# One more folded piece in the annex, eight more kept rows at the side, and a second pass in another order of groups and sizes (channel attention, 384x384x384)

## The chip, the cores and the metric

The kernel runs on one core of one Trainium2 chip. The metric is device time in microseconds (us) of one execution. Before the change: 716.69 us, the median of three runs (714.06, 716.69, 716.97).

## What is computed

The input `x` holds 384x384 positions of 384 channels in bf16 (113 MB). The reference takes the mean of each channel over all positions, multiplies it by the single weight `w1d[0]` (the 1D convolution has width k = 1), applies a sigmoid, and multiplies every position by the resulting 384 factors:

```python
g = jnp.einsum("bhwc->bc", x) / (H * W)
s = _sigmoid(g * w1d[0])          # k = 1: the loop over the window has one turn
return x * s[:, None, None, :]
```

The factors need all of `x`, so `x` must be read once in full before the first output can be written, and whatever cannot be held in on-chip memory must be read a second time.

## The kernel before

**Rows.** A "row" of the kernel is one position for each of the 128 partitions: 128 x 384 bf16, 98,304 bytes of HBM traffic when it is moved. `x` is 1152 rows. An instruction that the profile shows as 128x3072 works on 8 rows.

**Two passes.** Pass one loads all 1152 rows through the SP queue (`load`, L286) and lets TensorE add them into one PSUM bank (`sum_rows`, L292, a matmul with ones for each row). Of these, 392 rows stay on chip ("kept") and 760 are streamed: they pass through and are overwritten. ScalarE then makes the factors (`s_bf`, L516). Pass two scales the kept rows and stores them, loads the 760 streamed rows again, scales them (`scale`, L530, VectorE; three small pieces at the start on GpSimd) and stores them (`store`, L544). Loads and stores all go through the one SP queue, in program order.

**Memory.** The arena has 275 rows. A second area, the annex (20 rows, taken from the scratch of the descriptors), is numbered from X on. Before, the annex holds 20 raw kept rows, loaded at the start, and is only a buffer for streaming in pass two.

**Folding.** The exponent bits of the data have a small range, so the kernel packs 16 rows into the space of 12: `fold` (L343) takes pieces of 4 rows (three w and one u), moves the fields of u into unused bits of the three w, and frees the 4 rows of u. Each piece costs VectorE two tests (L359), four shifts and masks (`bits`, L327) and three joins (L333), and ScalarE two checks of 8 rows (L364). These share temporary rows (T and Y, 8 rows each), so one piece must finish before the next passes. The rows freed at the top of a group (U, V, W) and the temporary rows T and Y are loaded raw at the end of pass one. `unfold` (L548) takes a piece apart again in pass two: `fields` rebuilds u, `three` restores and scales the three w, `fourth` restores and scales u; both use T for halves. Pieces: FIRST (one), two columns of four groups of two pieces, BANKED (one piece of 6, whose words lie in PSUM banks during pass one) and EXTRA (one piece at A).

**Order.** In pass one, `BETWEEN` (L483) is written by hand: after which group which slots are streamed through; at L508 stands the order of the last raw loads. In pass two a planner runs while the program is built: it keeps a model clock and, by `RULES` (L650), `order` (L725) and the lists `landed` and `alongside`, decides at each moment whether VectorE unfolds a piece or scales landed rows, and when SP stores or loads, and how many rows at once. It writes a fixed sequence for each engine. On the chip a step waits only for what it needs: a load for the landing of the stores that free its rows, a store for its scaling, a scaling for the landing of its load. Since SP works in order, a waiting load also holds the stores behind it.

Of the kernel before, what the change touches and what calls it, by code (L numbers as in the profile page):

```python
# [145 lines left out]
def kernel(  # L146
# [13 lines left out]
    B, H, W, C = x.shape  # L160
# [5 lines left out]
    bf16, f32, u16, u32 = x.dtype, mybir.dt.float32, mybir.dt.uint16, mybir.dt.uint32  # L166
# [15 lines left out]
    ROWS = Y + 2 * PIECE  # L182


    FIRST = 0
    GROUPS = [(0, PIECE)]
    COLUMNS = ([FIRST], [])
# [11 lines left out]
    RING, SCRATCH = 1024, 16384  # L199
# [4 lines left out]
    X, N_X = ROWS + 1, (SCRATCH - RING) // (2 * C)  # L204
    END = X + N_X
    N_RAW = ROWS - W + 2 * PAIR + N_X
# [13 lines left out]
    arena = pool.tile([P, ROWS, C], bf16, name="arena")  # L220
# [22 lines left out]
    def mem(a, n):  # L243
        return arena[:, a : a + n, :] if a < X else annex[:, a - X : a - X + n, :]
# [8 lines left out]
    N_STREAM = RPP - N_RAW - 1 - sum(4 * q for _, q in GROUPS)  # L253
# [9 lines left out]
    r = N_STREAM + N_BANKED  # L263
# [7 lines left out]
    def raw(a):  # L271

        lo = a - U if a < G0 else PAIR + a - V if a < A else 2 * PAIR + a - W
        return c_raw + (lo if a < X else lo - (X - ROWS))
# [61 lines left out]
    def flat(a, p):  # L336
        return arena[:, a : a + p, :].bitcast(u16)
# [45 lines left out]
    N_DVE, N_SP = (62, 14), 27  # L383
# [45 lines left out]
    def take_raw(a, n):  # L429
        load(raw(a), a, n)  # L430
        return sum_rows(a, n)
# [7 lines left out]
    take_raw(X, N_X)  # L439
# [14 lines left out]
    SLOTS = [(A, 12), (A + 12, 12), (A + 24, 14)]  # L454
    S1, S2, S3 = ([slot] for slot in SLOTS)

# [8 lines left out]
    def group(g, where):  # L465
# [16 lines left out]
    LATE = [(W + 4, 8), (U, 8), (W + 12, 8), (W + 20, 7)]  # L482
    BETWEEN = [  # L483
        (2, LOW_COLUMN + HIGH), (4, [(A, 38)]),
        (5, [(G0 - 24, 24), (A - 24, 24), *S1]),
        (6, (S2, S3 + S1)), (7, ([(A - 24, 24)] + S2, S3 + S1)),
        (8, (S2 + S1, [(U, 8)] + S3)), (EXTRA, LATE),
    ]
# [59 lines left out]
    def unfold(g, lo, p, n, first, whole):  # L548

        a, at, m = first + 3 * lo, first + 3 * GROUPS[g][1] + lo, n * p  # L550
        folded = arena[:, a : a + 3 * m, :].rearrange("q (i j r) c -> q j i (r c)", i=n, j=3)
# [4 lines left out]
            arena[:, e : e + m, :].rearrange("q (i r) c -> q i (r c)", i=n).bitcast(u16)  # L556
# [64 lines left out]
    def again():  # L621
# [29 lines left out]
        (60, 190, 2.5, 14, 7.0, 5.0, 4.0),  # L651
        (150, 190, 2.5, 14, 5.0, 9.0, 3.0),
        (360, 72, 2.5, 33, 5.0, 7.0, 3.5),
        (N_STREAM, 220, 3.0, 14, 12.0, 7.0, 6.0),
# [43 lines left out]
    TOPS = {COLUMNS[0][-1]: U, COLUMNS[1][-1]: V, EXTRA: W}  # L698
# [11 lines left out]
    for a, n, end in ((Y, 2, True), (Y + 2, 2, True), (Y + 4, 4, True), (V, 4, True), (V + 4, 4, True), (T, 8, True), (X, 10, True), (X + 10, 10, True), (U, 8, True)):  # L710
        landed.append((a, raw(a), n, end))
    landed.append((W, raw(W), 8, True))
    landed.append((W + 8, raw(W + 8), 6, True))
# [14 lines left out]
    home[BANKED], home[EXTRA] = 2, 3  # L728
    free = [True] * 4
# [176 lines left out]
```

## Time and profile before

| | |
|---|---|
| profiled execution | 716.13 us |
| its span in the trace | 714.3 us |
| median of three runs | 716.69 us |
| moved by DMA | 301.34 MB, 422 GB/s over the span |
| HBM read / written | 187.96 / 113.25 MB |
| busy: PE / VectorE / ScalarE / GpSimd | 212.5 / 474.4 / 121.5 / 10.2 us |
| pass one ends (start of `s_bf`) | 268.65 us |
| first store of pass two issued | 269.85 us |

The 1.8 us between the profiled execution's time and its span lie outside what the trace shows. In the tables by windows each row gives, for 5 us, the busy time of each engine (with the number of instructions), then the granted clock of TensorE, the mean busy share of the 16 DMA engines and what they moved. The share can exceed 1.00 by a little, because packets are counted where they start.

### The profile page before, as it was taken

To read this page: it belongs to the slowest core of one execution; us is meant where nothing else is said; L and a number is where in the kernel's file an instruction comes from. 1 tells how busy PE (TensorE), PEld (TensorE's weight loads), DVE (VectorE), ACT (ScalarE), POOL (GpSimd) and SP (SyncE) were. 2 spreads that over 40 slices of the span, in tenths; PEclk is the share of its full clock that TensorE was granted. 3 is DMA by queue.
4 is the path that set the end of the run, shared out by engine and by line. 5 is a ranking of instruction groups with operands and counts; after the bars stand their busy time and mean duration, and the time that the engine had idled before them with its cause. 6 is when DMAs were issued, how large, how long until landed. Compare 5 with 4: busy or idle time off the path is not lost.

```text
span 714.3 us, 2033 instructions
## 1 busy us (share of the span) xinstructions
PE 212.5 (30%) x1186; PEld 0.3 (0%) x3; DVE 474.4 (66%) x350; ACT 121.5 (17%) x97; POOL 10.2 (1%) x7
## 2 busy tenths in 40 slices
PE   4768977997869780000000000000000000000000
PEld 0000000000000000000000000000000000000000
DVE  3605380639896827999989988999798388100960
ACT  3703260427675620000020000000000000000000
POOL 0000000000000005000000000000000000000000
PEclk9898989999999996555555555555555555555555
DMA  9999999999999998999999999999999999999997
GB/s 366 446 425 430 434 429 432 437 435 421 427 429 427 426 383 347 392 428 426 436 428 440 422 434 430 433 427 440 426 433 412 432 436 416 436 436 427 429 434 326
DMA packets 19454, 301.34 MB, mean 422 GB/s; under 512 B 2162, under 2 KB 2674, under 8 KB 7538
## 3 DMA queue, kind: packets, MB, share of 16 engines
q1 hardware_dynamic: 19440, 301.21, 99.0%
q8 instruction: 4, 0.07, 0.0%
q14 instruction: 8, 0.07, 0.0%
q10 hardware_dynamic: 2, 0.00, 0.0%
HBM read 187.96 MB, written 113.25 MB: 422 GB/s over the span
## 4 chain that ended last, share of the span: by engine, by line
DMA 69%; DVE 17%; PE 6%; ACT 2%; SPq 1%; issue 0%; DVEq 0%
DMA arena<-in_x_dram 47%; DMA out_dram<-arena 20%; DVE arena L530 11%; PE bank L292 6%; DVE arena L327 3%; ACT arena L364 2%; DVE annex L530 2%; DMA annex<-in_x_dram 2%; DMA out_dram<-annex 1%; DVE arena L333 1%; SPq L286 1%; ACT s_bf L516 0%; ACT bank L446 0%; DVEq L124 0%; SPq L901 0%
## 5 line engine op out<-in xcount | busy, mean ns | idle before, releaser
L530 DVE TENSOR_TENSOR arena<-arena,s_bf 128x4992 bf16<-128x4992 bf16 (+14 forms) x53 | 206.8, 3932 | 92.7 <-DMA arena<-in_x_dram 77.7
L292 PE MATMUL bank<-arena,ones 128*128 128x384 bf16 x1131 | 203.6, 341 | 46.3 <-DMA arena<-in_x_dram 45.6
L327 DVE TENSOR_SCALAR arena<-arena 128x1536 uint16<-128x1536 uint16 (+4 forms) x193 | 136.5, 761 | 109.0 <-DMA arena<-in_x_dram 93.9
L364 ACT ACTIVATE arena<-arena 128x3072 uint16<-128x3072 uint16 (+1 forms) x38 | 107.6, 2831 | 111.8 <-DVE arena L327 111.8
L333 DVE TENSOR_TENSOR arena<-arena 128x1536 uint16<-128x1536 uint16 (+3 forms) x81 | 106.3, 1312 | 9.9 <-PE bank L292 6.8
L610 PE MATMUL bank<-odd,ones 128*128 128x1 bf16 x1 | 0.2, 187 | 282.8 <-DVE odd L605 282.8
L446 ACT COPY arena<-bank 128x512 uint32<-128x512 uint32 (+3 forms) x9 | 4.5, 496 | 96.5 <-DMA out_dram<-arena 96.3
L530 DVE TENSOR_TENSOR annex<-annex,s_bf 128x3840 bf16<-128x3840 bf16 x8 | 16.9, 2152 | 1.9 <-DMA annex<-in_x_dram 1.9
L530 POOL TENSOR_TENSOR arena<-arena,s_bf 128x1536 bf16<-128x1536 bf16 (+1 forms) x3 | 10.0, 3352 | 269.2 <-ACT bank L520 269.2
L446 ACT COPY bank<-arena 128x512 uint32<-128x512 uint32 (+3 forms) x9 | 4.1, 490 | 26.4 <-PE bank L292 26.4
L530 DVE TENSOR_TENSOR arena<-arena,bank 128x1536 bf16<-128x1536 bf16 (+2 forms) x7 | 8.2, 1233 | 0.0
L364 ACT ACTIVATION_READ_ACCUMULATOR arena<-arena 128x1 f32 x38 | 7.1, 186 | 0.0
L292 PE MATMUL bank<-zeros,ones 128*128 128x384 bf16 x32 | 5.5, 326 | 0.0
L530 DVE TENSOR_TENSOR annex<-annex,bank 128x3840 bf16<-128x3840 bf16 x2 | 4.2, 2148 | 0.0
L292 PE MATMUL bank<-annex,ones 128*128 128x384 bf16 x20 | 3.4, 326 | 0.0
L516 ACT ACTIVATE s_bf<-bank,w_sc 128x384 bf16<-128x384 f32 x1 | 0.6, 581 | 13.6 <-PE bank L292 13.6
L306 PE MATMUL bank<-arena,ones 128*128 128x384 bf16 x1 | 0.5, 477 | 7.9 <-DMA arena<-in_x_dram 7.9
L874 ACT ACT_TABLE_LOAD x1 | 1.3, 1283 | 0.7 <-PEq L890 0.7
L396 DVE TENSOR_SCALAR w_sc<-bank 128x1 f32<-128x1 f32 x1 | 0.2, 159 | 1.1 <-PE bank L391 1.1
L386 DVE MEMSET ones<- 128x128 bf16 x1 | 0.2, 165 | 1.0 <-SPq L118 1.0
L391 PE MATMUL bank<-w_bf,ones 1*128 1x1 bf16 x1 | 0.2, 178 | 2.1 <-DMA w_bf<-in_w1d_dram 2.1
L614 DVE CAST odd_i<-bank 128x1 int32<-128x1 f32 x1 | 0.2, 158 | 0.3 <-PE bank L610 0.3
(11 smaller groups left out, 1.5 us busy)
## 6 DMA issues: line engine op xcount, KB each, us to landing
arena<-in_x_dram SPq DMA_DIRECT2D x16, 4608.0 KB, 30.6
out_dram<-arena SPq DMA_DIRECT2D x7, 4608.0 KB, 41.0
out_dram<-arena SPq DMA_DIRECT2D x7, 3072.0 KB, 25.1
arena<-in_x_dram SPq DMA_DIRECT2D x5, 3072.0 KB, 14.0
arena<-in_x_dram SPq DMA_DIRECT2D x13, 1152.0 KB, 18.6
arena<-in_x_dram SPq DMA_DIRECT2D x5, 2304.0 KB, 21.5
arena<-in_x_dram SPq DMA_DIRECT2D x3, 3744.0 KB, 18.9
out_dram<-arena SPq DMA_DIRECT2D x3, 3744.0 KB, 24.1
```

The lines of the kernel that those rows point to most:

```text
L286: lambda: nc.sync.dma_start(out=mem(a, hi - lo), in_=view(xf, *run)[:, lo:hi, :]),
L292: return pe.add_instruction(mybir.InstMatmult(name=nc.get_next_instruction_name(), ins=[pe.lower_ap(rhs), pe.lower_ap(ones[:])], outs=[pe. ...
L306: return nc.tensor.matmul(acc, lhsT=ones[:], rhs=mem(i, 1)[:, 0, :], start=first, stop=last)
L327: lambda: nc.vector.tensor_scalar(out=dst, in0=src, scalar1=s0, scalar2=s1, op0=op0, op1=op1),
L333: "DVE", lambda: nc.vector.tensor_tensor(out=dst, in0=a, in1=b, op=op), reads=reads, writes=writes
L364: lambda: nc.scalar.activation(out=y, in_=y, func=ACTF.Copy, accum_out=seen[:, 2 * k + i : 2 * k + i + 1]),
L386: fl.add("DVE", lambda: nc.vector.memset(ones[:], 1.0), writes=["ones"])
L391: lambda: nc.tensor.matmul(votes, lhsT=ones[0:1, :], rhs=w_bf[0:1, 0:1], start=True, stop=True),
L446: "ACT", lambda: nc.scalar.copy(dst.bitcast(u32), src.bitcast(u32)), reads=reads, writes=writes
L516: lambda: nc.scalar.activation(out=s_bf[:], in_=acc, func=ACTF.Sigmoid, scale=w_sc[:, 0:1]),
L530: lambda: vec.tensor_tensor(out=v, in0=v, in1=s[:, None, :].to_broadcast([P, n, C]), op=Op.mult),
L874: nc.scalar.preload_act_table(ACTF.Sigmoid)
```

## The change

It does three things.

1. A new folded group LATE: one piece (16 rows in 12) in the annex, at X, with its top at Z = X + 12; the last 8 rows of the annex are then raw kept rows. The annex is thereby no longer loaded at the start: in pass one it is a slot for streaming (three times all 20 rows), LATE's 16 rows come at the end, then the 8 raw ones.
2. EXTRA grows from one piece to two (32 rows in 24), so A to W holds 24 rows and its top at W has 8. Kept are 400 rows, streamed 752.
3. Pass two gets another order of groups, other first raw pieces (55 raw rows in place of 79), and other numbers in `RULES`. The streaming slots of pass one are cut anew, and SP's filler waits go from 27 to 26 pairs.

The core of the diff (three of the four rules are left out):

```diff
-    GROUPS.append((A, PIECE))
-    W = A + 3 * PIECE
+    GROUPS.append((A, PAIR))
+    W = A + 3 * PAIR
+    X, N_X = ROWS + 1, (SCRATCH - RING) // (2 * C)
+    LATE = len(GROUPS)
+    GROUPS.append((X, PIECE))
+    Z = X + 3 * PIECE
...
-    N_RAW = ROWS - W + 2 * PAIR + N_X
+    N_RAW = ROWS - W + 2 * PAIR + END - Z
...
-    take_raw(X, N_X)
...
-        (8, (S2 + S1, [(U, 8)] + S3)), (EXTRA, LATE),
+        (8, (S3, [(A + 12, 12), (W + 8, 7)])),
+        (EXTRA, (S3, [(U, 8), (V, 8), (W + 8, 7)])), (LATE, []),
...
-    for a, n in [(V, 8), *LATE, (W, 4), (T, 4), (T + 4, 4), (Y, 4), (Y + 4, 2), (Y + 6, 2)]:
+    for a, n in [(U, 8), (V, 8), (W + 8, 7), (W, 8), (Z + 4, 4), (Z, 4), (T, 4), (T + 4, 4), (Y, 4), (Y + 4, 2), (Y + 6, 2)]:
...
-        (60, 190, 2.5, 14, 7.0, 5.0, 4.0),
+        (45, 190, 1.5, 14, 12.0, 7.0, 5.0),
...
-    for a, n in ((A + 26, 4), (A + 30, 4), (A + 34, 5)):
+    for a, n in ((Z, 4), (Z + 4, 4), (W + 10, 5)):
...
-    order = [c0[-1], EXTRA, c0[-2], c0[-3], c1[-1], BANKED, c1[-2], c0[-4], c1[-3], FIRST, c1[-4]]
+    order = [c0[-1], c0[-2], c0[-3], c1[-1], c1[-2], EXTRA, c0[-4], FIRST, c1[-3], BANKED, LATE, c1[-4]]
```

The first place is SP's queue at the end of pass one, from the load of the last piece to be folded (128x6144, 16 rows) to the last load; f_PE, f_DVE and f_ACT name the engine that a load waits for. Before, that piece is EXTRA's; the first 128x1536 behind it is W (EXTRA's top), the next two are T, the last three Y:

```order
L286 DMA arena<-in_x_dram 128x6144 [waits f_PE]
L286 DMA arena<-in_x_dram 128x3072
L286 DMA arena<-in_x_dram 128x3072 [waits f_PE] x2
L286 DMA arena<-in_x_dram 128x2688 [waits f_PE]
L286 DMA arena<-in_x_dram 128x3072 [waits f_PE,f_DVE]
L286 DMA arena<-in_x_dram 128x3072 [waits f_PE] x3
L286 DMA arena<-in_x_dram 128x2688 [waits f_PE]
L286 DMA arena<-in_x_dram 128x1536 [waits f_DVE] x3
L286 DMA arena<-in_x_dram 128x1536 [waits f_ACT]
L286 DMA arena<-in_x_dram 128x768 x2
```

The same place after the change; the 16 rows are LATE's piece in the annex, the two annex loads of 128x1536 are the raw rows at Z + 4 and at Z (LATE's top), and the next two are T:

```order
L289 DMA annex<-in_x_dram 128x6144 [waits f_PE]
L289 DMA arena<-in_x_dram 128x3072 [waits f_PE] x2
L289 DMA arena<-in_x_dram 128x2688 [waits f_PE]
L289 DMA arena<-in_x_dram 128x3072 [waits f_DVE]
L289 DMA annex<-in_x_dram 128x1536
L289 DMA annex<-in_x_dram 128x1536 [waits f_PE,f_DVE]
L289 DMA arena<-in_x_dram 128x1536 [waits f_DVE] x2
L289 DMA arena<-in_x_dram 128x1536 [waits f_ACT]
L289 DMA arena<-in_x_dram 128x768 x2
```

Between the last piece to be folded and the first load that waits for its fold stood 70 rows (8, 8, 8, 7, 8, 8, 8, 8, 7, up to W); now 35 rows stand there (8, 8, 7, 8, 4, up to Z).

The second place is SP's queue early in pass two, from the last raw 128x3072 on; f_SP names the landing of an earlier transfer. Before:

```order
L544 DMA out_dram<-arena 128x3072 [waits f_DVE]
L544 DMA out_dram<-arena 128x2304 [waits f_DVE]
L286 DMA annex<-in_x_dram 128x7680 [waits f_SP18,f_SP20]
L286 DMA arena<-in_x_dram 128x4992 [waits f_SP16,f_SP19,f_SP22]
L544 DMA out_dram<-arena 128x4608 [waits f_DVE]
L286 DMA arena<-in_x_dram 128x3840 [waits f_SP23,f_SP0]
L286 DMA arena<-in_x_dram 128x3072 [waits f_SP14,f_SP15]
```

After:

```order
L545 DMA out_dram<-arena 128x3072 [waits f_DVE]
L545 DMA out_dram<-arena 128x768 [waits f_DVE]
L545 DMA out_dram<-arena 128x1920 [waits f_POOL]
L289 DMA annex<-in_x_dram 128x3072 [waits f_SP14,f_SP17]
L289 DMA arena<-in_x_dram 128x3072 [waits f_SP12,f_SP13]
L289 DMA arena<-in_x_dram 128x3072 [waits f_SP18]
L289 DMA arena<-in_x_dram 128x2688 [waits f_SP19,f_SP20]
L545 DMA out_dram<-arena 128x4608 [waits f_DVE]
```

The 128x4608 in both is the store of the first twelve unfolded rows. Ahead of it, 79 raw rows were stored and 33 loaded (20 and 13); now 55 are stored and 31 loaded (8, 8, 8 and 7).

The third place is VectorE at the start of pass two (L530 and L531 scale, L327 and L330 begin to unfold). Before:

```order
L530 TENSOR_TENSOR arena<-arena,s_bf 128x768 [waits f_PE,f_ACT]
L530 TENSOR_TENSOR arena<-arena,bank_72 128x768 [waits f_ACT]
L530 TENSOR_TENSOR arena<-arena,bank_72 128x1536 x3
L530 TENSOR_TENSOR arena<-arena,bank_72 128x3072
L530 TENSOR_TENSOR annex<-annex,bank_72 128x3840 x2
L530 TENSOR_TENSOR arena<-arena,bank_72 128x3072 x2
L530 TENSOR_TENSOR arena<-arena,s_bf 128x2304
L327 TENSOR_SCALAR arena<-arena 128x1536 [waits f_SP21]
```

After:

```order
L531 TENSOR_TENSOR arena<-arena,s_bf 128x768 [waits f_PE,f_ACT]
L531 TENSOR_TENSOR arena<-arena,bank_72 128x768 [waits f_ACT]
L531 TENSOR_TENSOR arena<-arena,bank_72 128x1536 x3
L531 TENSOR_TENSOR arena<-arena,bank_72 128x3072 x3
L531 TENSOR_TENSOR arena<-arena,bank_72 128x768
L330 TENSOR_SCALAR arena<-arena 128x1536 [waits f_SP16]
```

VectorE scales 42 raw rows in place of 66 before it unfolds the first piece. In the whole program the transfers through SP go from 135 to 144 (86 loads and 58 stores in place of 83 and 52), and the changes of direction between runs of loads and runs of stores from 21 to 33.

More of the change, by code (lines that the diff above doesn't have):

```diff
@@ L336, in flat @@
     def flat(a, p):
-        return arena[:, a : a + p, :].bitcast(u16)
+        return mem(a, p).bitcast(u16)
     SHL, SHR, AND, OR, XOR = (
@@ L453 @@
     PARTS = ((0, CUT, spare, "spare"), (CUT, C, tail, "bank0"))
-    SLOTS = [(A, 12), (A + 12, 12), (A + 24, 14)]
-    S1, S2, S3 = ([slot] for slot in SLOTS)
+    S1, S2, S3 = [(A, 19)], [(A + 19, 19)], [(X, N_X)]
     HIGH = [(A - 48, 48)]
@@ L550, in unfold @@
         a, at, m = first + 3 * lo, first + 3 * GROUPS[g][1] + lo, n * p
-        folded = arena[:, a : a + 3 * m, :].rearrange("q (i j r) c -> q j i (r c)", i=n, j=3)
+        folded = mem(a, 3 * m).rearrange("q (i j r) c -> q j i (r c)", i=n, j=3)
         w = [folded[:, j].bitcast(u16) for j in range(3)]
@@ L555, in unfold @@
         u, b, c = (
-            arena[:, e : e + m, :].rearrange("q (i r) c -> q i (r c)", i=n).bitcast(u16)
+            mem(e, m).rearrange("q (i r) c -> q i (r c)", i=n).bitcast(u16)
             for e in (at, HALVES, HALVES + m)
@@ L697 @@
     unused = set(range(HALVES, ROWS))
-    TOPS = {COLUMNS[0][-1]: U, COLUMNS[1][-1]: V, EXTRA: W}
+    TOPS = {COLUMNS[0][-1]: U, COLUMNS[1][-1]: V, EXTRA: W, LATE: Z}
     def stored(a, n):
@@ L707, in stored @@
         return f
[L710 to L713, printed above, removed]
+    for a, n in ((Y, 2), (Y + 2, 2), (Y + 4, 4), (V, 4), (V + 4, 4), (T, 8), (U, 8), (W, 8), (W + 8, 2)):
+        landed.append((a, raw(a), n, True))
     alongside = deque()
     t = 1.0
-    for a, n in ((A + 26, 4), (A + 30, 4), (A + 34, 5)):
+    for a, n in ((Z, 4), (Z + 4, 4), (W + 10, 5)):
         scale(a, n, "POOL", after=[copied])
@@ L724 @@
     (c0, c1), N_NEAR = COLUMNS, 2
-    order = [c0[-1], EXTRA, c0[-2], c0[-3], c1[-1], BANKED, c1[-2], c0[-4], c1[-3], FIRST, c1[-4]]
+    order = [c0[-1], c0[-2], c0[-3], c1[-1], c1[-2], EXTRA, c0[-4], FIRST, c1[-3], BANKED, LATE, c1[-4]]
     line = deque(order)
     home = {g: i for i, column in enumerate(COLUMNS) for g in column}
-    home[BANKED], home[EXTRA] = 2, 3
-    free = [True] * 4
+    home[BANKED], home[EXTRA], home[LATE] = 2, 3, 4
+    free = [True] * 5
     total = len(GROUPS)
```

18 lines of the change are left out of this document (8 added, 10 removed).

## The prediction

> **What bounds the kernel now.** I read the page's totals first, then the tables by windows, then the chain of waits and the timeline around the end of pass one. On the page:
>
> ```profile
> span 714.3 us, 2033 instructions
> PE 212.5 (30%) x1186; PEld 0.3 (0%) x3; DVE 474.4 (66%) x350; ACT 121.5 (17%) x97; POOL 10.2 (1%) x7
> DMA  9999999999999998999999999999999999999997
> q1 hardware_dynamic: 19440, 301.21, 99.0%
> DMA 69%; DVE 17%; PE 6%; ACT 2%; SPq 1%; issue 0%; DVEq 0%
> ```
>
> The 16 DMA engines carry packets for 99.0% of the span, 707 us of 714.3. No engine is above 66%. The 17% of VectorE in the chain is work beside a full queue: the DMA row shows a 9 almost everywhere. So what counts is the packets' time, plus the time in which the queue is empty. 301.21 MB in 707 us is 2.348 us per MB, or **0.231 us per row** of 98,304 bytes (3064 rows: 1152 read, 1152 written, 760 read again).
>
> Where is it empty? Stretches of the table by windows around the change of passes, then some of pass two:
>
> ```profile
> 255.00:260.00 5.00, 3.70 (x21) 0.00 (x0) 0.00 (x0) 0.03 (x1) 0.00 (x0) 1.00 1.02 424
> 265.00:270.00 5.00, 3.30 (x18) 0.00 (x0) 0.74 (x2) 0.90 (x2) 0.34 (x1) 1.00 0.30 115
> 270.00:275.00 5.00, 0.00 (x0) 0.00 (x0) 5.00 (x6) 0.00 (x0) 5.00 (x2) 0.70 0.83 328
> 275.00:280.00 5.00, 0.00 (x0) 0.00 (x0) 5.00 (x3) 0.00 (x0) 4.63 (x2) 0.50 1.02 424
> 280.00:285.00 5.00, 0.00 (x0) 0.00 (x0) 3.27 (x3) 0.00 (x0) 0.00 (x0) 0.50 1.03 428
> 285.00:290.00 5.00, 0.00 (x0) 0.00 (x0) 4.34 (x6) 0.00 (x0) 0.00 (x0) 0.50 1.03 382
> 295.00:300.00 5.00, 0.00 (x0) 0.00 (x0) 4.93 (x6) 0.00 (x0) 0.00 (x0) 0.50 0.99 345
> 320.00:325.00 5.00, 0.00 (x0) 0.00 (x0) 3.09 (x3) 0.00 (x0) 0.00 (x0) 0.50 1.00 423
> 440.00:445.00 5.00, 0.00 (x0) 0.00 (x0) 4.97 (x3) 0.00 (x0) 0.00 (x0) 0.50 1.01 435
> 445.00:450.00 5.00, 0.00 (x0) 0.00 (x0) 5.00 (x2) 0.00 (x0) 0.00 (x0) 0.50 1.01 435
> 550.00:555.00 5.00, 0.19 (x1) 0.10 (x1) 1.50 (x4) 0.00 (x0) 0.00 (x0) 0.50 1.00 374
> 595.00:600.00 5.00, 0.00 (x0) 0.00 (x0) 2.19 (x2) 0.00 (x0) 0.00 (x0) 0.50 0.81 317
> ```
>
> Between the passes the shares of 0.30 and 0.83 leave 3.50 + 0.85 = **4.35 us** empty. Beside that, four windows carry less than the 430 GB/s or so of the rest: 382, 345, 374 and 317, which is 0.6 + 1.0 + 0.7 + 1.3 = **3.5 us** lost. In three of them the share is about 1, so there the packets themselves take longer; nothing on an engine explains it.
>
> **The change part by part.**
>
> *Fewer rows.* 752 instead of 760 rows are read twice: 8 x 0.231 = **-1.85 us**. The page would show 300.42 MB instead of 301.21 on the main queue.
>
> *Nine more transfers* (144 instead of 135). Each has 128 packets, 8 per DMA engine. The window from 275 to 285, with transfers of 4 to 10 rows, moved 424 GB/s at a share of 1.02 and 428 at 1.03, so 2.41 us of packets per MB; 440 to 450, with long ones, 435 at 1.01: 2.32. The 0.09 us per MB go with about 200 packets per MB (some 5 KB each) instead of about 33 (30 KB), a difference of 10 per engine, so about 8 ns per packet. 9 x 8 x 8 ns = **+0.6 us**.
>
> *Two more folds in pass one*, with their 13-odd VectorE instructions and two ScalarE tests each. The last fold of before from the timeline, the end of pass one from the chain, and SP's first stores from the timeline (first column start, second duration):
>
> ```profile
> 247.22 1.90 DVE L327 TENSOR_SCALAR arena<-arena 128x3072 uint16<-128x3072 uint16 x3 [1.01 <-DMA arena<-in_x_dram]
> 252.17 2.76 ACT L364 ACTIVATE arena<-arena 128x3072 uint16<-128x3072 uint16 x1 [1.10 <-DVE arena L327]
> 252.99 1.94 DVE L333 TENSOR_TENSOR arena<-arena 128x1536 uint16<-128x1536 uint16 x2
> ```
>
> ```profile
> 267.15 1.47 PE bank L292 x8
> 268.63 0.02 issue
> 268.65 0.59 ACT s_bf L516
> 269.24 0.02 issue
> 269.26 5.28 DVE arena L530 x6
> ```
>
> ```profile
> 269.85 5.05 SPq L544 DMA_DIRECT2D out_dram<-arena  x7
> ```
>
> A fold lasts 247.22 to 254.93, **7.7 us**; its last look at the u rows ends where the two joins begin, after 5.8 us. That was hidden: 70 rows, 16.2 us of packets, lay between EXTRA's piece and the load at W, and VectorE was idle from 255 to 260. Now 35 rows, 35 x 0.231 = 8.1 us, lie between LATE's piece and the load at Z that waits for 5.8 us of its fold. To that comes the delay from last packet to seen landing and from issue to first packet. The change of passes gives the two together: 4.35 us empty, of which 267.15 to 269.85 (PE, ScalarE, first scaling), 2.7 us, is work; **1.65 us** is left. 5.8 + 1.65 = 7.45 < 8.1: Z comes in time by 0.65 us. The end of the fold releases the second half of T: 7.7 + 1.65 = 9.35 against 8.1 plus the 8 rows of Z and T (1.85) = 9.95. So no hole, if the fold starts when its piece lands. If VectorE is still at EXTRA's second piece, the hole grows one for one; that piece lands 39 rows (9.0 us) earlier and takes 7.7, so 1.3 us are in hand. I take **+0.1**, with 0 and +1.3 (a backlog of twice that slack) as ends. For the fold before, in the middle of the pass, other queued streams are the cover.
>
> *The first stores of pass two.* The order is now: 55 raw rows, loads of 31, then the first twelve unfolded rows. The last raw scaling and the first piece taken apart, from the timeline:
>
> ```profile
> 281.92 1.35 DVE L530 TENSOR_TENSOR arena<-arena,s_bf 128x2304 bf16<-128x2304 bf16 x1
> 285.59 1.50 DVE L327 TENSOR_SCALAR arena<-arena 128x1536 uint16<-128x1536 uint16 x3 [2.31 <-DMA out_dram<-arena]
> 287.12 1.95 DVE L333 TENSOR_TENSOR arena<-arena 128x1536 uint16<-128x1536 uint16 x2
> 288.99 1.35 DVE L327 TENSOR_SCALAR arena<-arena 128x4608 uint16<-128x4608 uint16 x1
> 290.38 2.56 DVE L530 TENSOR_TENSOR arena<-arena,s_bf 128x4608 bf16<-128x4608 bf16 x1
> ...
> 292.96 0.34 SPq L544 DMA_DIRECT2D out_dram<-arena  x1
> 293.40 0.86 SPq L286 DMA_DIRECT2D arena<-in_x_dram  x2
> 293.44 0.96 DVE L530 TENSOR_TENSOR arena<-arena,s_bf 128x1536 bf16<-128x1536 bf16 x1
> ```
>
> The piece takes 7.4 us from its start to its first store, 8.8 us (285.59 to 294.40) for its 16 rows. It started 2.31 us after VectorE was free, when the store of U's 8 rows had landed. Walk through the new order: packets resume near 271; 86 rows (55 stored, 31 loaded) keep the queue busy for 19.9 us, to 291. VectorE scaled 66 raw rows from 269.26 to 283.3, 0.21 us per row; 24 fewer take 5 us less, so it is free near 278.3. U's rows are then stored 36 rows into the queue and no longer 60 (24 x 0.231 = 5.5 us earlier, 280 at best); I take 282 for the start, since they are also scaled in between. Its twelve rows are issued near 289.5 and have packets about 1 us later, 290.5. That is 0.5 us in hand. From there a single piece costs VectorE 8.8, and the scaling of 16 rows loaded in its place 16 x 0.21 = 3.4, together 12.2 us; DMA needs 48 rows x 0.231 = 11.1. Each such piece drains the queue by 1.1 us; the first two groups, now four pieces (before: three), are taken so, later ones as pairs, which cost less. The loads that SP issues ahead refill it. I take **+0.2 us** of holes; the ends are 0 and the missing reserve, 24 rows x 0.231 = +5.5.
>
> *More changes of direction*, 33 instead of 21. Four slow windows (3.5 us) stand against 17 changes that cost nothing visible (320 to 325, with loads of 20 and 13 rows turning to stores: 423). In proportion it would be 12 x 3.5/21 = +2.0. But 595 to 600 lies within a run of long loads, so the link is weak; by the nearest rows, most are free. I take **+0.6**; the ends are -2.5 (the slow places not met) and +2.0.
>
> *Nothing:* the later BANKED group (its copies are on ScalarE, which is 17% busy); two filler waits less on SP (behind them lie some 6 us of queued loads); the first load, now without the annex (140 rows, 32 us, are queued before a load waits for TensorE); the final three loads and stores (43 rows at the end in both).
>
> Sum, against the profiled execution's 716.13: -1.85 + 0.6 + 0.1 + 0.2 + 0.6 = -0.35, so **715.8 us**. The median of the runs shown is 716.69, 0.56 above that execution, and one run is 2.6 below it; what a measurement of this kernel can tell from no change is about 0.5%, or 3.6 us. The term that the change is sure of is half of that.
>
> **The rivals.**
>
> *Early drought.* VectorE is the bound of the first 60 us of pass two. For it: 0.5 us in hand at 291 and 12.2 against 11.1 us; SP is in order, so a store that waits for a scaling holds the loads behind it, and VectorE waits for those. Against it: before, the same piece had 2.3 us to spare. It decides from the point where a piece with its reload takes over 11.1 us for more than two pieces in a row without a reserve. Price up to 5.5 us less what I took: 721.1. Slower.
>
> *Every change of direction costs*, in proportion: +1.4 on my sum, 717.2. Within 0.5%.
>
> *Every transfer pays its delay.* If the 1.65 us between packets and their neighbours were not covered for the nine added transfers, they would cost 9 x 1.65 = 14.9 instead of 0.6 us: 730.1. Slower. The window 275 to 285, with transfers of 0.4 to 1 MB at 424 to 428 GB/s, speaks against it: behind a full queue the delay does not show. The Trainium skill (DMA: Bandwidth & Descriptors, section Bandwidth) has this rule, to batch transfers to 1 MiB or more for 75% of peak; its section on the anatomy of a DMA puts the fixed part at about 2 us, by which the nine would be an estimated 18 us. By that rule the smaller transfers of pass two are a mistake; the trace disagrees as long as others are queued.
>
> *The slow places vanish.* They may be accidents of where reads and writes meet, and the new order meets elsewhere: -2.5 instead of +0.6, so 712.7. Faster. Against it: more places to meet.
>
> *The change does not do what it says:* if the bytes did not fall by 0.79 MB, the sum would be 717.6.
>
> **How the numbers follow.** My forecast with its near neighbours 0.77 (of these 0.15 for direction in proportion and 0.01 for the bytes); drought 0.14; a delay per transfer 0.01; vanishing slow places 0.08. So faster by over 0.5% 0.08, within 0.77, slower 0.15. The range reaches most of the vanishing below, 713.2, and the larger part of the drought above, 719.5; about 0.12 is left out.
>
> **What would show it.** The main queue carries 300.4 MB. The window with the end of LATE's fold shows a DMA share of 1; a share under 0.8 there means that Z waited. The change of passes stays near 4.35 us. Between 285 and 345 the shares stay near 1: if they fall to 0.9 or lower in several windows and SP's waits for VectorE's scaling grow, it is drought. If shares stay at 1 and GB/s falls below 400 in more than four windows, it is direction. Wrong would be the whole argument if the span moved by more than 3 us with the sum of packets and holes unchanged.

## The result and the profile after

The change makes the kernel slower: 718.75 us, the median of 20 runs (715.95 to 723.41), against 716.59 (714.06 to 717.89, 20 runs) before; the ratio is 1.0042 with the 95% interval 1.0028 to 1.0055, so +2.2 us; 715.8 us was forecast. The profiled execution of after took 722.76 us, 4 us over its median; where a number needs it, two more profiles of after (717.42 and 717.46 us) and a second of before (717.80) stand beside it.

The page of after, the same rows that the prediction shows of before:

```profile
span 721.0 us, 2103 instructions
PE 217.6 (30%) x1186; PEld 0.3 (0%) x3; DVE 500.4 (69%) x394; ACT 132.8 (18%) x105; POOL 10.2 (1%) x7
DMA  9999999999999997999999999999999999999997
q1 hardware_dynamic: 20736, 300.43, 98.7%
DMA 61%; DVE 24%; PE 10%; ACT 1%; SPq 0%; issue 0%; DVEq 0%
```

The bytes are those of the forecast (300.4 MB). The row of tenths looks almost as it did, and the busy share of the queue is a little lower (98.7% after 99.0%). In the chain the DMA's part fell by 8 points while VectorE's and TensorE's grew; that alone says little, since the fastest kernel of this record (deeper_full, below) has 55% for the DMA and 30% for VectorE. The windows of after, around the end of pass one and the start of pass two (the last three numbers are TensorE's clock, DMA share and GB/s):

```profile
245.00:250.00 5.00, 3.78 (x15) 0.00 (x0) 4.71 (x8) 3.69 (x4) 0.00 (x0) 0.73 1.01 425
250.00:255.00 5.00, 5.00 (x30) 0.00 (x0) 4.06 (x6) 2.86 (x2) 0.00 (x0) 0.93 1.03 415
255.00:260.00 5.00, 4.06 (x26) 0.00 (x0) 4.92 (x8) 3.59 (x3) 0.00 (x0) 1.00 0.85 263
260.00:265.00 5.00, 3.84 (x23) 0.00 (x0) 4.76 (x7) 3.90 (x3) 0.00 (x0) 1.00 1.01 414
265.00:270.00 5.00, 4.37 (x27) 0.00 (x0) 0.96 (x1) 1.07 (x2) 0.00 (x0) 1.00 1.01 367
270.00:275.00 5.00, 2.57 (x14) 0.00 (x0) 0.00 (x0) 0.35 (x1) 0.00 (x0) 1.00 0.37 139
290.00:295.00 5.00, 0.00 (x0) 0.00 (x0) 3.46 (x3) 0.00 (x0) 0.00 (x0) 0.50 0.88 327
295.00:300.00 5.00, 0.00 (x0) 0.00 (x0) 4.87 (x5) 0.00 (x0) 0.00 (x0) 0.50 1.02 338
```

In before, 255 to 260 moved 424 GB/s; here it moves 263. The chain of after in order of time (start, duration, what) says what the last loads of pass one waited for:

```profile
265.02 0.97 DVE annex L336
265.99 0.02 issue
266.01 0.33 SPq L289
266.34 0.04 issue
266.38 6.71 DMA arena<-in_x_dram
273.08 0.04 issue
273.13 1.50 PE bank L295 x8
274.63 0.02 issue
274.65 0.59 ACT s_bf L517
```

The last join of LATE's fold ends at 265.99, and 20 ns later SP issues a load that waited for it. From there a straight line leads to the factors at 274.65, 6.0 us later than in before (268.65). The chain names only the last link; the window that lost most, 255 to 260, lies ahead of it. In the two further profiles of after the factors start at 271.09 and 272.37, in that of before at 269.01.

What stands behind the factors: 721.0 - 274.65 = 446.35 us, and 444.5 and 443.3 in the other two; in before 445.65 and 447.0. By the means of these five profiles **pass one loses 3.9 us and pass two gains 1.6**. The sum, +2.3, is near the measured loss, but the parts are rough: the three profiles of after lie up to 3.6 us apart in pass one and 3.0 in pass two.

### The profile page after: what moved, and what is told of

Read it like the earlier page. It is cut to its first block, busy times and chain, and to the rows that moved or that the text cites. A ratio compares the mean times of both kernels' runs of the same rounds, so it can differ in the third digit from the quotient of the medians.

```text
span 721.0 us, 2103 instructions
## 1 busy us (share of the span) xinstructions
PE 217.6 (30%) x1186; PEld 0.3 (0%) x3; DVE 500.4 (69%) x394; ACT 132.8 (18%) x105; POOL 10.2 (1%) x7
## 3 DMA queue, kind: packets, MB, share of 16 engines
q1 hardware_dynamic: 20736, 300.43, 98.7%
## 4 chain that ended last, share of the span: by engine, by line
DMA 61%; DVE 24%; PE 10%; ACT 1%; SPq 0%; issue 0%; DVEq 0%
DMA arena<-in_x_dram 45%; DVE arena L531 17%; DMA out_dram<-arena 13%; PE bank L295 10%; DVE arena L330 4%; DMA annex<-in_x_dram 3%; DVE arena L336 2%; ACT arena L367 1%; DMA out_dram<-annex 1%; DVE annex L531 0%; DVE annex L336 0%; SPq L289 0%; DVE annex L330 0%; SPq L545 0%; ACT s_bf L517 0%
## 5 line engine op out<-in xcount | busy, mean ns | idle before, releaser
L531 DVE TENSOR_TENSOR arena<-arena,s_bf 128x6144 bf16<-128x6144 bf16 (+10 forms) x68 | 220.1, 3269 | 83.0 <-DMA arena<-in_x_dram 72.6
L330 DVE TENSOR_SCALAR arena<-arena 128x1536 uint16<-128x1536 uint16 (+4 forms) x205 | 143.5, 754 | 94.9 <-DMA arena<-in_x_dram 85.5
L295 PE MATMUL bank<-arena,ones 128*128 128x384 bf16 x1067 | 194.6, 345 | 39.8 <-DMA arena<-in_x_dram 39.2
L367 ACT ACTIVATE arena<-arena 128x3072 uint16<-128x3072 uint16 (+1 forms) x42 | 118.6, 2824 | 111.6 <-DVE arena L330 111.6
L336 DVE TENSOR_TENSOR arena<-arena 128x1536 uint16<-128x1536 uint16 (+3 forms) x87 | 112.8, 1296 | 14.3 <-PE bank L295 11.3
L295 PE MATMUL bank<-annex,ones 128*128 128x384 bf16 x84 | 17.8, 377 | 7.5 <-DMA annex<-in_x_dram 7.5
L531 DVE TENSOR_TENSOR annex<-annex,s_bf 128x3072 bf16<-128x3072 bf16 (+1 forms) x4 | 8.6, 2156 | 2.9 <-DMA annex<-in_x_dram 2.8
L531 POOL TENSOR_TENSOR annex<-annex,s_bf 128x1536 bf16<-128x1536 bf16 x2 | 6.2, 3108 | 275.2 <-ACT bank L521 275.2
L531 DVE TENSOR_TENSOR arena<-arena,bank 128x1536 bf16<-128x1536 bf16 (+2 forms) x8 | 8.6, 1144 | 0.0
L330 DVE TENSOR_SCALAR arena<-annex 128x1536 uint16<-128x1536 uint16 (+1 forms) x9 | 4.9, 599 | 0.2
L336 DVE TENSOR_TENSOR annex<-annex,arena 128x1536 uint16<-128x1536 uint16 (+1 forms) x4 | 4.6, 1156 | 0.2
L531 POOL TENSOR_TENSOR arena<-arena,s_bf 128x1920 bf16<-128x1920 bf16 x1 | 3.8, 3827 | 0.0
L309 PE MATMUL bank<-arena,ones 128*128 128x384 bf16 x1 | 0.5, 477 | 7.7 <-DMA arena<-in_x_dram 7.7
L330 DVE TENSOR_SCALAR annex<-annex 128x1536 uint16<-128x1536 uint16 (+1 forms) x3 | 2.5, 820 | 0.0
```

Of the source, the lines that this page charges most:

```text
L295: return pe.add_instruction(mybir.InstMatmult(name=nc.get_next_instruction_name(), ins=[pe.lower_ap(rhs), pe.lower_ap(ones[:])], outs=[pe. ...
L309: return nc.tensor.matmul(acc, lhsT=ones[:], rhs=mem(i, 1)[:, 0, :], start=first, stop=last)
L330: lambda: nc.vector.tensor_scalar(out=dst, in0=src, scalar1=s0, scalar2=s1, op0=op0, op1=op1),
L336: "DVE", lambda: nc.vector.tensor_tensor(out=dst, in0=a, in1=b, op=op), reads=reads, writes=writes
L367: lambda: nc.scalar.activation(out=y, in_=y, func=ACTF.Copy, accum_out=seen[:, 2 * k + i : 2 * k + i + 1]),
L531: lambda: vec.tensor_tensor(out=v, in0=v, in1=s[:, None, :].to_broadcast([P, n, C]), op=Op.mult),
```

## Experiments

Six questions, seventeen runs. A name that begins with p1 is a kernel without pass two: after the factors it scales and stores two rows and ends. "Rows on their way" at the issue of a load are the rows of all loads issued before it that have not landed. They are worked out from the start of each issue and from the completions in the trace, 16 to a load (one from each DMA engine), counted in order of time, whichever load they belong to. One row is 0.231 us of packets.

### Which pass loses?

`p1_before` and `p1_after` are the two kernels without pass two.

> The kernel before with pass two left out: after the factors, two rows are scaled and stored, and nothing else. It gives pass one's length alone. In the profile before, the factors begin at 268.65 us; the first scaling, one store and the end add some 6 us, so about 276 us. All theories expect the same here; the run is the base for the next two.

> The changed kernel with pass two left out in the same way. Theory A (the loss is made in pass one, where the changed streaming slots and the late fold leave SP's queue so shallow that DMA engines which are out of step run dry): longer than the kernel before without pass two by 2 to 6 us. Theory B (the loss is made in pass two, by more changes of direction and smaller transfers): within 0.7 us of it.

Measured: 275.30 us (274.70 to 275.68) and 277.56 us (276.70 to 278.84). The isolated pass one loses 2.3 us, less than the mean of the three profiles of whole kernels (3.9). That the loss lies ahead of the factors, both say; how much pass two gives back, they do not agree on: by these medians 0.1 us (718.75 - 277.56 against 716.59 - 275.30), by the profiles 1.6.

### Is it the size of the streaming slots?

`p1_fine` and, whole, `fine_full` cut the three slots of the change in two:

```diff
-    S1, S2, S3 = [(A, 19)], [(A + 19, 19)], [(X, N_X)]
+    S1, S2, S3 = [(A, 10), (A + 10, 9)], [(A + 19, 10), (A + 29, 9)], [(X, 10), (X + 10, 10)]
```

SP's filler waits go from 26 to 22 pairs with it.

> The changed kernel without pass two, and with the streaming slots of pass one cut in two (10 and 9 rows instead of 19, 10 and 10 instead of 20; six more loads, SP's filler waits down by four pairs to keep the same place). Theory A1 (the size of the slots is what makes TensorE and SP wait): at least 1 us shorter than the changed kernel without pass two. Theory A2 (LATE's fold, which now ends the pass, is what counts): no shorter than that, within 0.7 us. Theory B: all three within 0.7 us.

> The changed kernel with the streaming slots of pass one cut in two, and pass two unchanged. Theory A1: at least 1 us faster than the changed kernel, 716.5 to 717.5. A2 and B: as the changed kernel, 718 to 719.5.

Measured: 277.78 us (276.51 to 279.53), no better than the change; whole, 717.40 us, ratio to before 1.0018 (1.0005 to 1.0031). The whole kernel lies in theory A1's range, but its interval overlaps that of the change (1.0028 to 1.0055), and its pass one alone is not shorter, so the sizes are not shown to be a cause. (Nor did six more transfers cost anything like a delay of 1.65 us each.)

### Is it one place?

Four kernels. `p1_cover` streams 19 rows once more ahead of a load that waits at 213 to 219 us; `p1_nolate` leaves out LATE's fold; `p1_bless` was to take the rows at that first place out of before; `p1_early` loads and folds LATE at the start and has the slots of before.

```diff
-        (2, LOW_COLUMN + HIGH), (4, [(A, 38)]),
+        (2, LOW_COLUMN + HIGH), (4, [(A, 19)]),
...
-        (6, (S1, S2)), (7, ([(A - 24, 24)], S1)),
+        (6, (S1, S2)), (7, ([(A - 24, 24)] + S2, S1)),
```

That is p1_cover, against the change; p1_nolate, against the change:

```diff
-                fold(k)
+                if g != LATE:
+                    fold(k)
```

p1_bless, against before:

```diff
-        (2, LOW_COLUMN + HIGH), (4, [(A, 38)]),
+        (2, LOW_COLUMN + HIGH), (4, [(A, 38), (A, 19)]),
...
-        (6, (S2, S3 + S1)), (7, ([(A - 24, 24)] + S2, S3 + S1)),
+        (6, (S2, S3 + S1)), (7, ([(A - 24, 24)], S3 + [(A, 5)])),
```

And p1_early, against the change:

```diff
     take(BANKED)
+    take(LATE)
+    take_raw(Z + 4, 4)
...
+    for k in of_group(LATE):
+        fold(k, TEMPS, TEMPS + 2 * GROUPS[BANKED][1])
...
-    S1, S2, S3 = [(A, 19)], [(A + 19, 19)], [(X, N_X)]
+    S1, S2, S3 = [(A, 12)], [(A + 12, 12)], [(A + 24, 14)]
...
-        (6, (S1, S2)), (7, ([(A - 24, 24)], S1)),
-        (8, (S3, [(A + 12, 12), (W + 8, 7)])),
-        (EXTRA, (S3, [(U, 8), (V, 8), (W + 8, 7)])), (LATE, []),
+        (6, (S2, S3 + S1)), (7, ([(A - 24, 24)] + S2, S3 + S1)),
+        (8, (S3 + S1, [(U, 8)] + S2)),
+        (EXTRA, ([(U, 8), (W + 8, 7)], [(U, 8), (V, 8), (W + 8, 7)])),
```

Its last raw loads begin with four rows at Z, since Z + 4 is loaded at the start.

> The change's pass one alone (pass two left out: two rows scaled and stored), with the slot S2 (19 rows) streamed once more in group 7, ahead of the load that waits for the sums of a 24-row stretch, and 19 rows less after group 4; the same 1152 rows in all. The change without this edit took 277.56 us, the kernel before 275.30. Theory C (queue too short at 215 to 230 us, between the 24-row load and the 8-row load that waits for its sums: 43 rows in the change, 62 here as before): 276.2 to 276.8. Theory F (the wait for LATE's fold at the end costs it all): 277.3 to 277.8. If each has its part: 276.5 to 277.2, with a share near 1 from 215 to 230 us.

> The change's pass one alone (pass two left out), and LATE's sixteen rows are loaded and summed but not folded (that work is left out), so that the last loads wait for EXTRA's fold, 8 us earlier. Theory F (the wait for LATE's fold at the end costs it all): 275.3 to 275.8. Theory C (the short queue at 215 to 230 us): 277.2 to 277.8. If each has its part: 276.2 to 277.0, with 255 to 265 us at a share near 1 and 215 to 230 us as low as it was.

> The pass one of before alone (pass two left out), with S2 (19 rows... 12 in this kernel's slot plus 7) taken out ahead of the waiting load in group 7, so that 43 rows stand there as in the change, and 19 rows more after group 4. Without the edit 275.30 us. Theory C: 276.0 to 276.8, with a share under 1 near 215 to 230 us. Theory F: 275.1 to 275.6, since the end of pass one is untouched.

> The change's pass one alone (pass two left out), with 400 kept rows as in the change, but LATE's sixteen rows loaded and folded at the start of the program and the annex not used for streaming; the slots and their order as before (12, 12 and 14 rows). Theories C and F both: 275.2 to 275.8, as before, since neither the short queue nor the late fold is left. A third (the extra fold itself, 8 us more of VectorE in pass one, or the 24 more rows in folds, costs the time wherever it stands): 277.0 to 277.8.

Measured: 278.22 (277.42 to 278.69), 277.73 (276.82 to 279.20), 283.6 (282.65 to 285.02) and 278.01 us (277.19 to 278.64). Neither single place brought anything back: p1_nolate came out in theory C's range, but p1_cover, which was to settle C, is slower than any theory gave it. p1_early, where both theories forecast the time of before, was as slow as the change. So for a while the third theory (the extra fold costs the time wherever it stands) was ahead. The windows of p1_early pointed elsewhere:

```profile
245.00:250.00 5.00, 3.98 (x23) 0.00 (x0) 4.89 (x8) 3.69 (x3) 0.00 (x0) 1.00 0.98 372
250.00:255.00 5.00, 3.35 (x20) 0.00 (x0) 4.81 (x6) 3.97 (x3) 0.00 (x0) 1.00 0.97 385
255.00:260.00 5.00, 3.63 (x21) 0.00 (x0) 3.90 (x7) 3.05 (x4) 0.00 (x0) 1.00 0.93 318
260.00:265.00 5.00, 2.31 (x14) 0.00 (x0) 0.00 (x0) 0.00 (x0) 0.00 (x0) 1.00 0.92 333
```

The time is lost at the end of pass one, as in the change, though LATE's fold is at the start. What is left there is EXTRA's second piece and its slots U, V and W + 8, each used again soon after its last use. So it is not one place: every kernel of this group has some load that waited and was issued with few rows on their way.

p1_bless was badly made, since its second use of A stands directly behind the first, but its windows show the pure case:

```profile
160.00:165.00 5.00, 4.22 (x26) 0.00 (x0) 4.61 (x7) 3.79 (x3) 0.00 (x0) 1.00 0.95 402
165.00:170.00 5.00, 3.30 (x21) 0.00 (x0) 4.64 (x6) 3.80 (x4) 0.00 (x0) 1.00 0.03 12
170.00:175.00 5.00, 3.04 (x19) 0.00 (x0) 3.65 (x6) 2.86 (x2) 0.00 (x0) 1.00 0.84 295
```

The first use has landed in full at 166.20; the load behind it, of 19 rows, is issued at 169.98, with 0 rows on their way, when TensorE has summed the 38 rows; its first completion comes at 175.80. Less 4.4 us for its own packets, the issue adds 1.4 us: the first packet starts 0.96 us after the issue began, and the first packets of each engine take up to 1.0 us longer than the 0.545 us of the later ones. With its share of 0.03 the hole is plain; of the place that was meant (230 us) it says nothing.

### Few rows on their way, or the extra piece?

`p1_short` is before without pass two, with every fold as before; only 15 of the 31 rows streamed behind EXTRA's fold move to the first part of pass one. `p1_deep` is p1_early with the eight rows at Z as one more place for streaming.

```diff
+    ENDS = [(W + 4, 8), (U, 8)]
...
-        (8, (S2 + S1, [(U, 8)] + S3)), (EXTRA, LATE),
+        (8, (S2 + S1, [(U, 8)] + S3)), (EXTRA, ENDS),
```

The raw loads at the end stay as they are. p1_deep, against p1_early (with Z loaded at the end, and W in two halves), and deep_full, the same with pass two:

```diff
-        (EXTRA, ([(U, 8), (W + 8, 7)], [(U, 8), (V, 8), (W + 8, 7)])),
+        (EXTRA, ([(U, 8), (W + 8, 7)], [(Z, 8), (U, 8), (V, 8), (W + 8, 7)])),
```

> The pass one of before alone (pass two left out), with 392 kept rows and every fold as before; of the four streamed slots after EXTRA's fold only (W + 4, 8) and (U, 8) stay, and the other 15 rows are streamed in the first part of pass one. So at the first raw load that uses W + 4 again some 8 rows are on their way, at the next two 16; before, never under 20. Without the edit 275.30 us. Theory D: 276.3 to 277.5, with shares near 0.9 between 253 and 265 us. Theory X: 275.0 to 275.6, since nothing is added.

> The change's pass one alone (pass two left out), LATE's sixteen rows loaded and folded at the start as in the run p1_early, and now the eight rows of its top are a place for streaming too (after EXTRA's second piece) and are loaded at the end, in two halves like W. By the times at which loads are issued and land, p1_early had 11 to 12 rows on their way at four issues between 248 and 259 us; here at least 20 are to be there at each. Theory D (what costs the 2.3 us is that fewer than some 20 rows, 4.6 us, are on their way when a load that waited is issued): 275.4 to 276.3. Theory X (the extra piece costs the time wherever it stands, by its VectorE work, its loads or memory traffic): 277.5 to 278.3.

> The whole kernel with the pass one of the run p1_deep and the change's pass two. Theory D: pass one is as fast as before, pass two as it was measured for the change (441.2 us), so 716.4 to 717.4, no difference from before that can be told; the ratio to before 0.999 to 1.001. Theory X: 718.0 to 719.3, as the change.

Measured: p1_short 277.41 us (277.11 to 277.64), **+2.1 us with no fold, row or byte added**. Theory X gave at most 275.6 here; few rows on their way are enough for such a loss. Its windows:

```profile
250.00:255.00 5.00, 4.67 (x29) 0.00 (x0) 4.39 (x6) 2.86 (x2) 0.00 (x0) 1.00 0.90 373
255.00:260.00 5.00, 3.44 (x21) 0.00 (x0) 3.06 (x5) 2.86 (x2) 0.00 (x0) 1.00 0.84 273
260.00:265.00 5.00, 2.56 (x16) 0.00 (x0) 0.00 (x0) 0.00 (x0) 0.00 (x0) 1.00 1.00 382
```

The middle one is close to the window of the change that lost most (0.85 and 263). p1_deep took 276.43 us (276.10 to 278.26), just over the upper end of theory D's range: half of the loss was back, and three issues still had 12 to 16 rows ahead of them. Whole, deep_full: 716.42 us, ratio 1.0015 (0.9994 to 1.0037), so no difference from before that can be told.

### With more rows still

`p1_deeper` and, whole, `deeper_full`, against p1_deep:

```diff
-        (EXTRA, ([(U, 8), (W + 8, 7)], [(Z, 8), (U, 8), (V, 8), (W + 8, 7)])),
+        (EXTRA, ([(U, 8), (W + 8, 7), (Z, 8)], [(V, 8), (U, 8)])),
...
-    for a, n in [(Z, 4), (Z + 4, 4), (U, 8), (V, 8), (W + 8, 7), (W, 4), (W + 4, 4), (T, 4), ...
+    for a, n in [(W + 8, 7), (W, 4), (Z, 4), (Z + 4, 4), (V, 8), (U, 8), (W + 4, 4), (T, 4), ...
```

> The change's pass one alone (pass two left out), LATE early as in p1_deep, with 8 rows fewer streamed after EXTRA's second piece and the places Z, V and U each used in an order that leaves more rows between two uses, so that some 24 or more rows are on their way at each issue after 225 us (p1_deep: 12 to 16 at three issues between 254 and 258 us, 276.43 us). Theory D (fewer than some 20 rows on their way is what costs): 275.3 to 275.9. Theory X (the extra piece itself costs the rest): 276.2 to 276.8, as p1_deep.

> The whole kernel with the pass one of p1_deeper and the change's pass two. If pass one is as before and pass two saves what p1_deep and deep_full together showed (440.0 us against 441.3): 715.0 to 715.9, ratio to before 0.998 to 0.9995. If pass two is worth what it was in the change (441.2 us): 716.4 to 717.1. If the rest of pass one's loss stays: 716.2 to 717.8.

Measured: p1_deeper **275.57 us** (274.98 to 276.63), the time of before with the extra pieces folded and 400 rows kept, so theory X is out. The rows on their way fell to 16 once (257 us), not as high as expected, and that was enough. Its windows at the end of pass one:

```profile
250.00:255.00 5.00, 3.70 (x23) 0.00 (x0) 3.45 (x5) 2.58 (x3) 0.00 (x0) 1.00 1.00 415
255.00:260.00 5.00, 4.54 (x28) 0.00 (x0) 4.84 (x7) 3.91 (x4) 0.00 (x0) 1.00 1.05 415
260.00:265.00 5.00, 3.43 (x20) 0.00 (x0) 0.02 (x1) 0.11 (x2) 0.00 (x0) 1.00 0.99 401
```

deeper_full took **714.69 us** (713.35 to 718.53), ratio to before 0.9980 (0.9966 to 0.9994): 1.6 us under the before that was timed beside it (716.33), by 0.2%, and 4.1 under the change's median. It lies below all three forecasts. Its page:

```profile
span 712.4 us, 2105 instructions
DMA  9999999999999997999999999999999999999997
q1 hardware_dynamic: 21456, 300.43, 99.1%
```

The rows on their way, over the kernels without pass two (issues from 210 us to the last load of pass one):

```
kernel      lowest counts, in rows     issues under 18   median us
p1_before   20 22 23 23 23 24           0                275.30
p1_deeper   16 19 20 20 20 22           1                275.57
p1_deep     12 15 16 19 20 20           3                276.43
p1_short     8  8 16 20 24 31           3                277.41
p1_nolate   15 16 23 24 27 31           2                277.73
p1_after    12 12 12 15 16 16           8                277.56
p1_fine      8  8 12 12 14 16           6                277.78
p1_early    11 12 12 16 20 20           4                278.01
p1_cover    12 15 16 16 16 16           6                278.22
```

With at least 16 to 20 rows on their way (3.7 to 4.6 us) the loads of these kernels that waited cost next to nothing (p1_deeper, +0.3 us); with 8 to 15 at the lowest, pass one lost 1.1 to 2.9 us. The numbers hang on how a landing is counted: by each load's own 16 completions the lowest counts are 23 in p1_before, 27 in p1_deeper, 20 in p1_deep and 8 to 16 in the other six, which is the same order of good and bad. The price isn't a plain function of the count: p1_nolate has only two short issues and loses as much as the change, and in its profile TensorE ran at a clock of 0.53 while LATE's load waited for its sums:

```profile
245.00:250.00 5.00, 5.00 (x18) 0.00 (x0) 4.12 (x6) 3.97 (x3) 0.00 (x0) 0.53 0.96 399
250.00:255.00 5.00, 5.00 (x33) 0.00 (x0) 3.58 (x5) 2.08 (x3) 0.00 (x0) 1.00 0.95 350
255.00:260.00 5.00, 4.54 (x28) 0.00 (x0) 1.96 (x3) 2.01 (x2) 0.00 (x0) 1.00 0.93 328
```

A slow TensorE clock is thus a rival for a part of the loss, in the change too: the clock was 0.73 from 245 to 250 us in after, and 0.66 close ahead of the holes of after_b and after_c. There TensorE took 0.30 us for a row (12 sums from 247.77 us in after), and packets bring one in 0.231. But it isn't needed: p1_short and p1_early lost 2.1 and 2.7 us at a clock of 1.00 from 225 us on, and before still moved 422 GB/s from 215 to 220 us at 0.76. How much the clock adds in the change was not tried.

### The rules of pass two, and where the time lies

`oldrules` is the change with the four `RULES` of before. `after_b`, `after_c` and `before_b` are the unchanged kernels again, for their profiles.

> The change, with the four rules of the planner as they stood before (pass one is that of the change). If the new numbers of the rules are what keeps pass two from giving the 1.1 us of packets that eight rows fewer save: 717.0 to 718.0. If the order of groups and the fewer raw rows at the start do it: 718.5 to 719.5. If the new numbers serve the new order: over 719.5.

> The change as it is, for a second profile. If pass two saves nothing and pass one loses 2.3 us: the factors start at 270.5 to 272.0 and the rest takes 445 to 446.5. If pass two saves 2 us and pass one loses 4 to 5: the factors start at 273 to 274.7 and the rest takes 443 to 444.

> A third profile of the change, with the same two possibilities: factors at 270.5 to 272.0 and 445 to 446.5 behind them, or factors at 273 to 274.7 and 443 to 444 behind them.

> A second profile of the kernel before: the factors at 268.5 to 269.3 and 445 to 446 behind them; if its first profile was unlucky in pass two, 443 to 444.5.

Measured: oldrules 726.10 us, ratio to before 1.0134 (1.0112 to 1.0155), 7.4 us worse than the change, so the new numbers serve the new order. Two windows show where: VectorE is busy throughout and the queue runs out behind it, while after_c moves 423 and 428 GB/s there.

```profile
445.00:450.00 5.00, 0.00 (x0) 0.00 (x0) 5.00 (x3) 0.00 (x0) 0.00 (x0) 0.50 0.74 278
455.00:460.00 5.00, 0.00 (x0) 0.00 (x0) 5.00 (x2) 0.00 (x0) 0.00 (x0) 0.50 0.93 334
```

after_b: factors at 271.09 and 444.5 us behind them; after_c: 272.37 and 443.3. Neither of the two possibilities held in both numbers; it lies between. Three other kernels with the change's pass two (fine_full, deep_full, deeper_full) have 443.6, 443.0 and 443.2 us behind the factors; before_b has 447.0 and was no luckier than the first profile of before.

## Why the prediction was wrong

**Bytes and packets** (-1.85 and +0.6) were right. 300.43 MB were moved. In before the median packet of every size but one takes 8.5 ns and 0.03677 ns per byte, to within 1 ns. At this price its main queue needs 702.6 us, that of after 701.4: -1.1 against -1.25. What the profiles show above this price says where the rest went. In pass one, as a mean of the 16 engines, packets took 1.1 and 1.4 us more than it in before, and 4.8, 2.6 and 3.5 in the three profiles of after; the engines carried nothing for 2.8 and 2.8 us, against 5.3, 3.9 and 4.2.

**Two more folds in pass one (+0.1) is the step that failed.** It rests on two sentences. The first, "Z comes in time by 0.65 us", set 35 rows, 8.1 us, against 5.8 us of fold and 1.65 of delay. The fold itself was as forecast; from VectorE's timeline of after:

```profile
258.27 1.90 DVE L330 TENSOR_SCALAR arena<-annex 128x3072 uint16<-128x3072 uint16 x3
...
264.04 1.94 DVE L336 TENSOR_TENSOR annex<-annex,arena 128x1536 uint16<-128x1536 uint16 x2
```

7.7 us, begun 0.4 us after the piece had landed. What was too small is the delay. I took it from the change of passes, where one small transfer follows another on engines that are in step. In the middle of a long queue they are not: the 16 engines complete the last load ahead of Z 1.4 us apart in after and after_c and 2.1 in after_b, so the leading ones run out early. With this the sum would be 8.9 to 9.6 us against 8.1 for Z, and 10.8 to 11.5 against 9.95 for T. In after_b this is what happened: Z's load is issued at 262.47, when the first engine had completed everything ahead of it (262.05), and the window moved 276 GB/s:

```profile
260.00:265.00 5.00, 5.00 (x33) 0.00 (x0) 4.27 (x7) 2.86 (x2) 0.00 (x0) 1.00 0.78 276
```

In after it did not: an earlier hole had held up the rows ahead of Z, so Z's load (264.15) was issued 2.0 us before the first engine had completed the load ahead (266.14), and 260 to 265 moved 414 GB/s. And p1_nolate, where nothing waits for LATE's fold, loses as much as the change. So this sentence alone doesn't explain the loss.

The second, "for the fold before, in the middle of the pass, other queued streams are the cover", gave no price to the newly cut slots of pass one and to the loads that wait for TensorE's sums of them, and it weighs more. The rows ahead of a waiting load fell from 20 to 12 and 15 (p1_after at 218 and 248 us). The largest hole of after, 255 to 260, is of this kind: the load of U's 8 rows was issued at 254.66, after waiting for TensorE's sums, with nothing but LATE's 16 rows on their way. By p1_cover and p1_nolate neither place alone accounts for the loss; with more rows at every such load (p1_deeper) 2.0 of the 2.3 us are gone, and short issues alone, in before, make 2.1 (p1_short). In place of +0.1 the runs show **+2.3** (kernels without pass two) to +3.9 (mean of the profiles).

**The first stores of pass two** (+0.2) were near. The windows of after_c:

```profile
285.00:290.00 5.00, 0.00 (x0) 0.00 (x0) 4.90 (x5) 0.00 (x0) 0.00 (x0) 0.50 0.91 331
290.00:295.00 5.00, 0.00 (x0) 0.00 (x0) 3.16 (x3) 0.00 (x0) 0.00 (x0) 0.50 1.01 358
295.00:300.00 5.00, 0.00 (x0) 0.00 (x0) 4.97 (x5) 0.00 (x0) 0.00 (x0) 0.50 0.99 385
```

Against the 430 GB/s of the rest these lose 2.5 us (2.5 and 2.8 in after and after_b); the same three of before (382, 425 and 345 GB/s) lose 1.6, so about +1. No drought of the size of that rival came: between 285 and 345 us one window of the three profiles has a share of 0.9 or less (0.88, in after). The change of passes stayed near its 4.35 us (5.05, 4.0 and 4.7).

**Changes of direction** (+0.6) went the other way. The rival that the slow places vanish was in part right: the same 60 us, 550 to 610, of before, then of deeper_full, then of after_c:

```profile
550.00:610.00 60.00, 0.19 (x1) 0.10 (x1) 40.53 (x8) 0.00 (x0) 0.00 (x0) 0.50 1.01 423
```

```profile
550.00:610.00 60.00, 0.19 (x1) 0.10 (x1) 59.48 (x31) 0.00 (x0) 0.00 (x0) 0.50 1.01 434
```

```profile
550.00:610.00 60.00, 0.18 (x1) 0.10 (x1) 59.48 (x30) 0.00 (x0) 0.00 (x0) 0.50 1.01 434
```

11 of 430 GB/s over 60 us are 1.5 us, in the new order's favour. That the new order is the reason is not shown: the first profile of after loses 2.9 us between 400 and 450 us (405 GB/s), where the other two move 427 and 431. In before at 550.79 a load that had waited was issued with 16 rows on their way, so the slow window at 550 is of the same kind as those in pass one. The one at 595 lies in a queue of 176 rows and stays unexplained.

**A delay per transfer**, the rule of the Trainium skill (DMA: Bandwidth & Descriptors, the anatomy of a DMA: a fixed part of about 2 us for each, given there for transfers issued from GpSimd, while these come from SP), is now better placed. p1_deeper has three transfers more than p1_before and is 0.27 us longer, so behind a full queue the delay does not show, as forecast. But it is there (1.4 us in p1_bless), and together with engines out of step it sets how much must be queued ahead.

**"The window with the end of LATE's fold shows a DMA share of 1"** was a test of Z alone, and its answer is mixed: the fold ends at 265.99, 264.30 and 264.38 us, and the window that holds its end has a share of 1.01 in after, 0.78 in after_b and 0.98 in after_c. The hole of after lies earlier, where the test didn't look. The GB/s was the better witness, since the packets behind a hole take longer, up to 1.0 us in p1_short and 1.7 in after, and are counted as busy: p1_short has a share of 1.00 at 382 GB/s. So the windows of before with a share of 1 and few GB/s, which I called slow packets, were partly the same thing (550 to 555).

## What to carry to other kernels

For each load that waits for an engine, count the rows already on their way when it can be issued, and ask for the delay that an issue adds (1.4 us) plus the spread of the DMA engines (2.0 to 2.4 us at the end of pass one in before and p1_before), not for the wait alone; here that is some 4 us, 16 to 20 rows. More data kept on chip can take its room from the buffers that hold this reserve, so a change that saves traffic can lose it again at the end of the pass, where nothing comes behind. There the order in which places are used again was worth more than the bytes (2.0 us from p1_after to p1_deeper, against 1.1 us of packets). Read GB/s beside the busy share, because the share counts the slow packets behind a hole as work.

## What the runs showed of the hardware

- A packet of the main queue takes 8.5 ns plus 0.03677 ns per byte: 65 ns for 1536 bytes, 1364 for 36,864 (before, medians).
- The 16 engines drift apart in steps. First and last completion of one load lie 1.38 us apart in the first 40 us of before and 2.29 from 50 us on; in the profile of after it is 3.06 from 46 us and 3.89 at 172, then 2.2 from 218 us and 1.4 at 257. Soon after the queue has run empty between the passes it is 0.15 us (before, at 277 us). What makes the steps was not settled: instruction fetches (queue 8 of the trace) lie near some of them, but the first stands at 56.9 us in before, after its step.
- Engines in step may need less: in before, stores between 272 and 277 us are issued with 4 to 8 rows on their way, and the window 275 to 280 still moved 424 GB/s at a share of 1.02.
- A load on an empty queue: its first packet starts 0.96 us after the issue began, and 1.4 us are added to the time of its packets in all (p1_bless at 169.98 us).
